# Two pairs of weight sums formed one run earlier, and an empty step ahead of a batch's scores

## The chip, the cores and the metric

The kernel runs on one core of one Trainium2 chip. The metric is the time of one execution on the device in microseconds (us), lower is better. Times of a kernel are the median of several runs; traces come from one profiled execution.

## The reference

Eight batches with 8 heads, 576 tokens and a head dimension of 64. Keys and values are averaged over groups of 8 tokens, the attention is formed over the 72 averages, and its result (4608 tokens by 512) goes through a feed-forward layer 512 -> 2048 -> 512 with a leaky ReLU of slope 0.01. All in float32.

```python
k_p = k.reshape(B, H, Sp, pool, D).mean(axis=3)
v_p = v.reshape(B, H, Sp, pool, D).mean(axis=3)
scores = scale * np.matmul(q, k_p.transpose(0, 1, 3, 2))
scores = scores - np.max(scores, axis=-1, keepdims=True)
attn = np.exp(scores)
attn = attn / (np.sum(attn, axis=-1, keepdims=True) + 1e-09)
attn_out = np.matmul(attn, v_p)
...
h = x @ w_in
g = np.maximum(0.01 * h, h)
return (g @ w_out).astype(np.float32)
```

## The kernel before, in words

**Work.** The feed-forward layer takes the tokens in nine chunks of 512 (the four tiles of 128 of a chunk). Every factor is split into a high and a low part, so a product takes three matmuls. `m1` (L1131) forms one block of 128 of the 2048 hidden columns for a chunk: 12 matmuls (L1143 to L1145) into a bank `ph` of which there are two in turn, Prelu on ScalarE (L1148), the high part `gh` on ScalarE (L1151), the low part `gl` on VectorE (L1152). `m2` (L1156) adds such a block, two blocks later, to the four accumulators `acc`: 12 matmuls (L1354 to L1356 in `add_up`). Between two `yield`s lie six matmuls; this is a beat.

**Runs.** `runs` lists twelve stretches: run 0 is chunk 0 with hidden blocks 0 to 7, runs 1 and 2 chunk 1 with blocks 0 to 7 for half the tiles each, run 3 chunk 1 with blocks 8 to 15, run 4 (`REST`) chunk 0 with blocks 8 to 15, which is the first chunk's second half, and runs 5 to 8 are the third to the sixth chunk whole. The last three chunks are computed by another scheme with seven products in place of eight, which needs sums and differences of quarters of the weights. For each of eight pairs of hidden blocks these sums are formed beforehand and kept in DRAM (`kept`) by `prepare` (L1172).

**prepare.** A pair takes seven steps with nine additions on VectorE (L1183) into a scratch tile `x_tail`, four casts to the high part on ScalarE (`high`, L1186) and four differences for the low part on VectorE (`low`, L1190). The eight parts lie in `places`, which `free` (L1223) gives: upper halves of the columns of the x tiles (`xh`, `xl`) of a chunk that is not filled yet. Behind the seventh step eight transfers of 128 KB (L1217) and, for the first few pairs, one of 256 KB (L1220) write them to `kept` from SP's queue. `PLAN` (L1513) says for each run how many pairs it forms, from which beat and until which.

**Attention beside it.** The attention of the next batches is cut into steps that are issued between the beats: `ku` makes the pooled keys transposed (`kT`, L484 and L489, VectorE), `q` the queries (L565), `s` the scores of half the heads of a tile (`pss`, L600) with the maximum (L608, VectorE) and the exps (L610, ScalarE), `sb` the normalised rows `at` (L640 and L641 on VectorE, L644 and L650 on GpSimd, called POOL in the profile), which SP writes to DRAM (`rows`, L661) and reads back in another layout (`blocks`, L670). `pu` transposes the blocks (`pp`, L681, VectorE) and splits them (`pT_hi` L703 on ScalarE, `pT_lo` L706 and a masked `pT_hi` L710 on VectorE), `au` multiplies by the values (`pa`, L725 to L728) and copies the result to the x tiles (`xh` L744, `xl` L745). A batch's tiles go through `pu` and `au` in pieces. The first twelve steps of batch 2 are put at the end of run 3 (L1499), behind twelve empty steps.

**Outputs.** When a tile of a run has all its blocks, `store` (L1394 and around) copies its accumulator to `o`, one half on ScalarE and one on VectorE, and SP stores it; buffers `o` and `pp` share a pool of five.

**Order.** TensorE's instructions are issued in the order in which the program is written. Up to the last three chunks the order on the other engines and on SP is set by a scheduler, from dependences and estimated times.

Of the kernel before, what the change touches and what calls it, by code (L numbers as in the profile page):

```python
# [10 lines left out]
F32 = mybir.dt.float32  # L11
# [13 lines left out]
def tile_pooled_attention_ffn(  # L25
# [9 lines left out]
    nc = tc.nc  # L35
# [36 lines left out]
    HALF = CH // 2  # L72
# [679 lines left out]
    def x_parts(c):  # L752

        if c not in xs:
            side = c if c < 2 else (c + 1) % 2
            xs[c] = [
                [one.tile([P, CH], F32R, tag=f"x{w}{side}_{kk}", name=f"x{w}{c}_{kk}") for kk in range(NK)]
                for w in "hl"
            ]
        return xs[c]  # L760
# [285 lines left out]
    def line_up_pinned(pieces, ahead, fresh):  # L1046
# [73 lines left out]
    runs = [  # L1120
        (0, range(SPLIT), FULL), (1, range(SPLIT), FULL[:2]), (1, range(SPLIT), FULL[2:]),
        (1, range(SPLIT, NF), FULL), (0, range(SPLIT, NF), FULL),
    ]
    REST = len(runs) - 1
# [45 lines left out]
    kept = dram.tile([len(PAIRS), P, 5, 2, HALF], F32, name="kept")  # L1170

    def prepare(j, places):  # L1172

        f0, f1 = PAIRS[j]
        (a11, a12), (a21, a22) = (
            [[ws[0, f].bitcast(F32)[:, part, half] for part in range(2)]
             for half in (slice(0, HALF), slice(HALF, DM))] for f in (f0, f1)
        )
        u, w = (x_tail[:, 2 * i : 2 * i + 2, :].rearrange("p k x -> p (k x)") for i in range(2))
        ADD, SUB = ALU.add, ALU.subtract  # L1180

        def do(out, a, b, op):
            nc.vector.tensor_tensor(out, a, b, op=op)  # L1183

        def high(i, of):
            nc.scalar.copy(places[i][0], of)  # L1186

        def low(i, of):
            h, l = places[i]
            nc.vector.tensor_tensor(l, of, h.bitcast(F32), op=SUB)  # L1190

        do(u, a21[0], a21[1], ADD)
        do(w, u, a22[0], ADD)
        yield
        do(w, w, a22[1], ADD)
        high(1, w)
        do(u, a11[0], u, SUB)
        yield
        do(u, u, a11[1], ADD)
        high(0, u)  # L1200
        low(1, w)
        yield
        do(w, w, a11[0], SUB)
        low(0, u)
        yield
        do(w, w, a11[1], SUB)
        high(2, w)
        do(u, a12[0], w, SUB)
        yield
        do(u, u, a12[1], ADD)  # L1210
        high(3, u)
        low(2, w)
        yield
        low(3, u)
        for i, parts_of in enumerate(places):
            for k, part in enumerate(parts_of):
                nc.sync.dma_start(kept[j, :, i, k, :], part.bitcast(F32))  # L1217
        if j < OPEN:
            with tc.issue_after(sent[-1].ins):
                nc.sync.dma_start(kept[j, :, 4], ws[0, f1].bitcast(F32)[:, :, HALF:])  # L1220
        yield

    def free(n, i):  # L1223

        if n < REST + FAST - 2:
            return [(h[:, HALF:], l[:, HALF:]) for h, l in zip(*x_parts(runs[n][0] + 1))]
        side, part = (runs[n][0] + 2) % 2, "hl"[i % 2]
        x = [one.tile([P, CH], F32R, tag=f"x{part}{side}_{kk}", name=f"place{i}_{kk}") for kk in range(NK)]
        return [(y[:, :HALF], y[:, HALF:]) for y in x]
# [251 lines left out]
    for n, pieces in enumerate(beside):  # L1481
        us = [att[b][u] for b, u in line_up([x for x in pieces if x[0] < VIA])]
        us += [
            att[x[0]][x[1]] if x else lambda: None
            for x in line_of(n, [x for x in pieces if x[0] >= VIA])
        ]
        if n == 0:

            cut = us.index(att[1]["au01"]) + 1
            us, rest = us[:cut], us[cut:]  # L1490

            us.remove(att[1]["sa20"])
            us.insert(us.index(att[1]["au00"]) + 1, att[1]["sa20"])
            us = [att[0][u] for u in TAIL_STEPS.split()] + us
        elif n == 1:
            us = rest
        if n == REST:

            units[-1] = [lambda: None] * AHEAD + us[:AHEAD]  # L1499
            us = us[AHEAD:]  # L1500
        units.append(us)
# [8 lines left out]
    for b, n in loads_at.items():  # L1510
        early[max(n, REST) - 1].append(b)

    PLAN = {REST + 1: (2, 10, 36), REST + 2: (3, 3, 34), REST + 3: (1, 3, 20), REST + 4: (2, 3, 34)}  # L1513
    STEPS_OF = 7
    left = list(range(len(PAIRS)))

    def sums_in(n):
        for i in range(PLAN[n][0]):
            yield from prepare(left.pop(0), free(n, i))

    at = 0
    for n, (c, fs, ts) in enumerate(runs[: REST + FAST - 1]):
        us = list(units[n])
# [12 lines left out]
        beats, done, beat = (2 + len(ts) // 2) * len(fs), 0, 0  # L1536
        forming, formed = (sums_in(n), 0) if n in PLAN else (None, 0)
        many, begin, until = PLAN.get(n, (0, 0, 1))
        behind = 10 if final else 4
# [43 lines left out]
    for part in (at - 2, at - 1):  # L1583
        n, c, f = parts[part]
# [12 lines left out]
    for n in range(REST + FAST - 1, len(runs)):  # L1597
        c = runs[n][0]
        us = list(units[n])
# [61 lines left out]
```

## Time and profile before

| | |
|---|---|
| median of 3 runs | 916.63 us (916.19 to 918.4) |
| the profiled execution | 919.39 us |
| its span in the trace | 917.6 us |
| mean granted TensorE clock | 0.991 |
| TensorE busy | 886.1 us, 97% |
| VectorE / ScalarE / GpSimd busy | 56% / 49% / 24% |

The profile is one execution; its span runs from the first to the last instruction, and the execution's time is 1.8 us longer. In rows of instructions the first two numbers are the start from the span's start and the duration, `<-` stands between what is written and what is read, and in brackets stand the idle time before and what ended it. Matmuls overlap, so that one shows 0.39 us though the next starts 0.23 us after it. The clock is given as a share of 2.4 GHz.

### The profile page before, as it was taken

How to read it: one execution, taken by the hardware profiler on the slowest of the kernel's cores; microseconds unless marked ns; L12 is line 12 of the kernel's file. 1: busy time of each engine (PE TensorE's matmuls, PEld its weight loads, DVE VectorE, ACT ScalarE, POOL GpSimd, SP SyncE). 2: the span in 40 equal slices, each digit the busy share in tenths (PEclk: the TensorE clock that was granted, in tenths of full speed). 3: DMA queues.
4: the chain of work that ended last, by engine and by line, in shares of the span. 5: the costliest groups of instructions: out<-in, count | busy, mean ns of one | idle time of the engine just before them, and what ended most of it. 6: DMA issues, size and time to landing. Idle time of an engine off the chain costs nothing.

```text
span 917.6 us, 14146 instructions
## 1 busy us (share of the span) xinstructions
PE 886.1 (97%) x4731; PEld 764.1 (83%) x4731; DVE 515.8 (56%) x1229; ACT 447.4 (49%) x1397; POOL 223.6 (24%) x394
## 2 busy tenths in 40 slices
PE   5599999999999999999999999999999999999998
PEld 4478888788887888888888888888999999999997
DVE  6999569546276654774465537655665653342222
ACT  5788559345344534443454336354654553453322
POOL 4511110352534231412133132514320230010000
PEclk9889999999999999999999999999999999999999
DMA  9965231327357342834245317630785255425332
GB/s 266 313 203 171 64 76 47 88 61 197 102 163 169 109 96 53 230 93 109 53 141 118 97 36 195 162 102 3 198 212 148 67 148 144 122 78 161 104 113 72
DMA packets 157464, 116.53 MB, mean 127 GB/s; under 512 B 100688, under 2 KB 136016, under 8 KB 157392
## 3 DMA queue, kind: packets, MB, share of 16 engines
q1 hardware_dynamic: 145488, 90.86, 36.7%
q10 hardware_dynamic: 11904, 24.78, 9.4%
q8 instruction: 37, 0.61, 0.3%
q14 instruction: 35, 0.29, 0.1%
HBM read 85.07 MB, written 30.54 MB: 126 GB/s over the span
## 4 chain that ended last, share of the span: by engine, by line
PE 84%; DVE 7%; ACT 3%; DMA 2%; POOL 1%; issue 1%; SPq 1%; POOLq 0%; DVEq 0%; ACTq 0%
PE acc L1354 13%; PE acc L1355 13%; PE acc L1356 13%; PE ph L1143 8%; PE ph L1144 8%; PE ph L1145 8%; PE ends_y L1261 7%; PE ends_x L1261 6%; PE pss L600 3%; DMA kremraw<-in_k_dram 1%; PE pa L726 1%; DMA blocks<-rows 1%; PE pa L728 1%; PE pa L727 1%; PE pa L725 1%
## 5 line engine op out<-in xcount | busy, mean ns | idle before, releaser
L1354 PE MATMUL acc<-w,gh 128*128 128x512 f32 x576 | 228.2, 396 | 0.7 <-DVE o L1394 0.7
L1355 PE MATMUL acc<-w,gh 128*128 128x512 f32 x576 | 225.9, 392 | 0.0
L1356 PE MATMUL acc<-w,gl 128*128 128x512 f32 x576 | 225.0, 391 | 0.0
L1143 PE MATMUL ph<-xh,w 128*128 128x512 f32 (+1 forms) x416 | 159.5, 384 | 0.6 <-DVE gl L1152 0.6
L1144 PE MATMUL ph<-xl,w 128*128 128x512 f32 (+1 forms) x416 | 156.5, 376 | 0.0
L1145 PE MATMUL ph<-xh,w 128*128 128x512 f32 (+1 forms) x416 | 156.3, 376 | 0.0
L1356 PEld LDWEIGHTS acc<-w,gl 128*128 128x128 f32 x576 | 108.4, 188 | 23.5
L1354 PEld LDWEIGHTS acc<-w,gh 128*128 128x128 f32 x576 | 108.7, 189 | 20.1 <-issue 1.1
L1355 PEld LDWEIGHTS acc<-w,gh 128*128 128x128 f32 x576 | 108.7, 189 | 18.1
L610 ACT ACTIVATE e<-pss,red 128x72 f32<-128x72 f32 (+1 forms) x320 | 97.8, 329 | 44.6 <-DVE red L608 44.5
L1148 ACT ACTIVATE ph<-ph 128x512 f32<-128x512 f32 (+1 forms) x104 | 57.7, 555 | 94.8 <-PE ph L1145 94.3
L1152 DVE TENSOR_TENSOR gl<-ph,gh 128x512 fp32r<-128x512 f32 (+1 forms) x104 | 66.8, 642 | 61.3 <-ACT gh L1151 60.8
L644 POOL TENSOR_TENSOR at<-e,red 128x128 f32<-128x128 f32 (+1 forms) x120 | 50.1, 438 | 173.9 <-DVE red L641 90.9
L1143 PEld LDWEIGHTS ph<-xh,w 128*128 128x128 f32 x416 | 79.2, 190 | 14.6 <-DVE gl L1152 1.2
L1145 PEld LDWEIGHTS ph<-xh,w 128*128 128x128 f32 x416 | 79.0, 190 | 14.3
L1144 PEld LDWEIGHTS ph<-xl,w 128*128 128x128 f32 x416 | 79.1, 190 | 13.1
L610 ACT ACTIVATION_READ_ACCUMULATOR e<-pss,red 128x1 f32 (+1 forms) x320 | 68.6, 214 | 0.0
L681 DVE STREAM_TRANSPOSE pp<-blocks 128x384 f32<-128x384 f32 (+1 forms) x60 | 44.2, 758 | 41.2 <-DMA blocks<-rows 41.2
L608 DVE TENSOR_REDUCE red<-pss 128x4 f32<-128x288 f32 (+1 forms) x80 | 35.8, 453 | 52.9 <-PE pss L600 51.5
L703 ACT CAST pT_hi<-pp 128x384 fp32r<-128x384 f32 (+1 forms) x80 | 36.8, 479 | 52.5 <-DVE pp L681 48.7
L1151 ACT CAST gh<-ph 128x512 fp32r<-128x512 f32 (+1 forms) x104 | 57.8, 556 | 2.6
L600 PEld LDWEIGHTS pss<-kT,qT 128*128 128x128 f32 x320 | 45.8, 195 | 8.4 <-ACT qT L577 2.2
(290 smaller groups left out, 1486.2 us busy)
## 6 DMA issues: line engine op xcount, KB each, us to landing
seat<-kept ACTq DMA_DIRECT2D x31, 512.0 KB
rows<-at SPq DMA_DIRECT2D x48, 192.0 KB
blocks<-rows SPq DMA_DIRECT2D x48, 192.0 KB
out_dram<-o SPq DMA_DIRECT2D x34, 256.0 KB
w_bits<-in_moe_w_in_dram SPq DMA_DIRECT2D x16, 512.0 KB
w_bits<-in_moe_w_out_dram SPq DMA_DIRECT2D x16, 512.0 KB
q<-in_q_dram SPq DMA_DIRECT2D x96, 64.0 KB
w<-kept ACTq DMA_DIRECT2D x21, 256.0 KB
```

Of the source, the lines that this page charges most:

```text
L600: nc.tensor.matmul(sc[:, 2 * SP * i : 2 * SP * (i + 1)], qT[:, p, :], kT[:, p, :, :].rearrange("d i s -> d (i s)"), start=True, stop=True,)
L610: ins = nc.scalar.activation(e[:n, h, :], scv[:n, h, :], AF.Exp, bias=mx[:n, h : h + 1], accum_out=sm[:n, h : h + 1],)
L1143: nc.tensor.matmul(ph, w[:, 0, ks], xh[kk][:, r], start=kk == 0, stop=False)
L1144: nc.tensor.matmul(ph, w[:, 0, ks], xl[kk][:, r], start=False, stop=False)
L1145: nc.tensor.matmul(ph, w[:, 1, ks], xh[kk][:, r], start=False, stop=kk == NK - 1)
L1148: nc.scalar.activation(ph, ph, AF.Prelu, alpha=0.01)
L1151: casts.append(nc.scalar.copy(gh, ph))
L1152: lows.append(nc.vector.tensor_tensor(gl, ph, gh.bitcast(F32), op=ALU.subtract))
L1261: nc.tensor.matmul(out, w[:, stay, ks], move, start=start and i + n == 0, stop=i + n == 3, skip_group_check=True,)
L1354: nc.tensor.matmul(a, gh[:, r], hi, start=first, stop=False)
L1355: nc.tensor.matmul(a, gh[:, r], lo, start=False, stop=False)
L1356: nc.tensor.matmul(a, gl[:, r], hi, start=False, stop=last)
```

## The change

Three edits. `low` issues the two transfers of a part right behind its difference, and the eight transfers at the end of `prepare` go; `free` is written so that run 4 too finds the tiles of the next chunk. In run 4's list of attention steps an empty step is inserted at index 2, behind twelve empty ones, so that it lies ahead of the first scores of batch 2. And `PLAN` gives two pairs to run 4 (beats 1 to 14), one instead of two to run 5 (beats 3 to 17 instead of 10 to 36), two instead of three to run 6 (from beat 7 instead of 3); runs 7 and 8 stay.

```diff
@@ prepare
         def low(i, of):
             h, l = places[i]
             nc.vector.tensor_tensor(l, of, h.bitcast(F32), op=SUB)
+            for k, part in enumerate(places[i]):
+                nc.sync.dma_start(kept[j, :, i, k, :], part.bitcast(F32))
...
         low(3, u)
-        for i, parts_of in enumerate(places):
-            for k, part in enumerate(parts_of):
-                nc.sync.dma_start(kept[j, :, i, k, :], part.bitcast(F32))
@@ free
-            return [(h[:, HALF:], l[:, HALF:]) for h, l in zip(*x_parts(runs[n][0] + 1))]
+            return [(h[:, HALF:], l[:, HALF:]) for h, l in zip(*x_parts(n - REST + 2))]
@@ the steps of run 4
         if n == REST:
 
+            us.insert(2, lambda: None)
             units[-1] = [lambda: None] * AHEAD + us[:AHEAD]
             us = us[AHEAD:]
...
-    PLAN = {REST + 1: (2, 10, 36), REST + 2: (3, 3, 34), REST + 3: (1, 3, 20), REST + 4: (2, 3, 34)}
+    PLAN = {REST: (2, 1, 14), REST + 1: (1, 3, 17), REST + 2: (2, 7, 34), REST + 3: (1, 3, 20), REST + 4: (2, 3, 34)}
```

What it does to the order stands below at three places. A row names line, operation, what is written and what is read; the last number of a name is a tile's own and differs between the two kernels.

TensorE, in run 3, where the first scores of batch 2 (`pss_0_0`, `pss_0_1`) stand; before:

```order
L1356 MATMUL acc_3_1694<-w_10_1698,gl_10_1977 128x512
L600 MATMUL pss_0_0_2135<-kT,qT_0_2122 128x144 x2
L600 MATMUL pss_0_1_2145<-kT,qT_0_2122 128x144 x2
L1143 MATMUL ph_13_2155<-xh_0_1073,w_13_1847 128x512
L1144 MATMUL ph_13_2155<-xl_0_1077,w_13_1847 128x512
```

And with the change:

```order
L1355 MATMUL acc_3_1694<-w_10_1698,gl_10_1977 128x512
L1143 MATMUL ph_13_2135<-xh_0_1073,w_13_1847 128x512
L1144 MATMUL ph_13_2135<-xl_0_1077,w_13_1847 128x512
L1145 MATMUL ph_13_2135<-xh_0_1073,w_13_1847 128x512
L1143 MATMUL ph_13_2135<-xh_1_1074,w_13_1847 128x512
L1144 MATMUL ph_13_2135<-xl_1_1078,w_13_1847 128x512
L1145 MATMUL ph_13_2135<-xh_1_1074,w_13_1847 128x512
L600 MATMUL pss_0_0_2142<-kT,qT_0_2122 128x144 x2
L600 MATMUL pss_0_1_2152<-kT,qT_0_2122 128x144 x2
L1143 MATMUL ph_13_2135<-xh_2_1075,w_13_1847 128x512
```

The scores stand six matmuls later, in the middle of `ph_13`. The second tile's move in the same way.

TensorE, at the start of run 4, where the third tile's scores stand; before:

```order
L1145 MATMUL ph_8_2340<-xh_3_394,w_8_1108 128x512
L600 MATMUL pss_2_0_2366<-kT,qT_2_2267 128x144 x2
L600 MATMUL pss_2_1_2376<-kT,qT_2_2267 128x144 x2
L1143 MATMUL ph_9_2386<-xh_0_391,w_9_1193 128x512
L1144 MATMUL ph_9_2386<-xl_0_395,w_9_1193 128x512
```

With the change:

```order
L1145 MATMUL ph_8_2345<-xh_3_394,w_8_1108 128x512
L1143 MATMUL ph_9_2380<-xh_0_391,w_9_1193 128x512
L1144 MATMUL ph_9_2380<-xl_0_395,w_9_1193 128x512
L1145 MATMUL ph_9_2380<-xh_0_391,w_9_1193 128x512
L1143 MATMUL ph_9_2380<-xh_1_392,w_9_1193 128x512
L1144 MATMUL ph_9_2380<-xl_1_396,w_9_1193 128x512
L1145 MATMUL ph_9_2380<-xh_1_392,w_9_1193 128x512
L600 MATMUL pss_2_0_2387<-kT,qT_2_2274 128x144 x2
L600 MATMUL pss_2_1_2397<-kT,qT_2_2274 128x144 x2
L1143 MATMUL ph_9_2380<-xh_2_393,w_9_1193 128x512
```

`ph_9`, which takes the bank that `ph_15` had, now follows `ph_8` directly; the scores come six matmuls later.

VectorE, in run 4, from the low part of the last block of run 3 (`gl_15`) on; `x_tail` is the scratch tile of the sums, `w_0` and `w_4` are weights, `red` the maxima and sums of the softmax. Before:

```order
L1152 TENSOR_TENSOR gl_15_2297<-ph_15_2274,gh_15_2296 128x512
L608 TENSOR_REDUCE red_2_0_2370<-pss_2_0_2366 128x4
L608 TENSOR_REDUCE red_2_1_2380<-pss_2_1_2376 128x4
L565 STREAM_TRANSPOSE qT_4_2838<-q_4_2269 128x2x4x32
L1152 TENSOR_TENSOR gl_8_2363<-ph_8_2340,gh_8_2362 128x512
L640 TENSOR_TENSOR red_2_0_2370<-red_2_0_2370,tiny 128x4
L641 RECIPROCAL red_2_0_2370<-red_2_0_2370 128x4
L640 TENSOR_TENSOR red_2_1_2380<-red_2_1_2380,tiny 128x4
L641 RECIPROCAL red_2_1_2380<-red_2_1_2380 128x4
L1152 TENSOR_TENSOR gl_9_2401<-ph_9_2386,gh_9_2400 128x512
L681 STREAM_TRANSPOSE pp_0_0_2428<-blocks_0_0_2426 128x4x96
L1394 COPY o_0_2415<-acc_0_1381 128x256
```

With the change:

```order
L1152 TENSOR_TENSOR gl_15_2289<-ph_15_2267,gh_15_2288 128x512
L1183 TENSOR_TENSOR x_tail<-w_0_336 128x256
L1183 TENSOR_TENSOR x_tail<-x_tail,w_0_336 128x256 x2
L1183 TENSOR_TENSOR x_tail<-w_4_657,x_tail 128x256
L1183 TENSOR_TENSOR x_tail<-x_tail,w_4_657 128x256
L1190 TENSOR_TENSOR xl_1_2329<-x_tail,xh_1_2325 128x256
L1152 TENSOR_TENSOR gl_8_2365<-ph_8_2345,gh_8_2364 128x512
L1183 TENSOR_TENSOR x_tail<-x_tail,w_4_657 128x256
L1190 TENSOR_TENSOR xl_0_2328<-x_tail,xh_0_2324 128x256
L608 TENSOR_REDUCE red_2_0_2391<-pss_2_0_2387 128x4
L608 TENSOR_REDUCE red_2_1_2401<-pss_2_1_2397 128x4
L565 STREAM_TRANSPOSE qT_4_2890<-q_4_2276 128x2x4x32
```

Between `gl_15` and `gl_8` stand five sums and a difference of the first pair, behind it more; up to the last `pT_hi` of the first piece (`pp_1_0`) it is ten sums and four differences, and `gl_10` has come ahead of that too.

ScalarE at the same place, before:

```order
L1151 CAST gh_15_2296<-ph_15_2274 128x512
L1148 ACTIVATE ph_8_2340<-ph_8_2340 128x512
L1151 CAST gh_8_2362<-ph_8_2340 128x512
L610 ACTIVATE e_2_0_2369,red_2_0_2370<-pss_2_0_2366,red_2_0_2370 128x72 x4
L610 ACTIVATE e_2_1_2379,red_2_1_2380<-pss_2_1_2376,red_2_1_2380 128x72 x4
L1148 ACTIVATE ph_9_2386<-ph_9_2386 128x512
```

With the change:

```order
L1151 CAST gh_15_2288<-ph_15_2267 128x512
L1186 CAST xh_1_2325<-x_tail 128x256
L1186 CAST xh_0_2324<-x_tail 128x256
L1148 ACTIVATE ph_8_2345<-ph_8_2345 128x512
L1151 CAST gh_8_2364<-ph_8_2345 128x512
L610 ACTIVATE e_2_0_2390,red_2_0_2391<-pss_2_0_2387,red_2_0_2391 128x72 x4
L610 ACTIVATE e_2_1_2400,red_2_1_2401<-pss_2_1_2397,red_2_1_2401 128x72 x4
L1148 ACTIVATE ph_9_2380<-ph_9_2380 128x512
L1186 CAST xh_2_2326<-x_tail 128x256
L1392 COPY o_0_2429<-acc_0_1381 128x256
```

Two casts of the first pair (L1186) stand ahead of `ph_8`'s Prelu, a third ahead of the first output copy.

## Rows read from the trace of the kernel before

**Rows 1.** The page: the span, and each engine's busy time in us.

```profile
span 917.6 us, 14146 instructions
...
PE 886.1 (97%) x4731; PEld 764.1 (83%) x4731; DVE 515.8 (56%) x1229; ACT 447.4 (49%) x1397; POOL 223.6 (24%) x394
```

**Rows 2.** TensorE's waits, 160 to 640 us: us in total, times, longest.

```profile
PE pa L726 <- DVE pT_lo L706: 2.1, 1, 2.1
PE pss L600 <- DVE kT L489: 1.1, 1, 1.1
PE acc L1354 <- DVE o L1394: 0.7, 1, 0.7
```

**Rows 3.** Windows: us, busy PE, PEld, DVE, ACT, POOL; clock, DMA share, GB/s.

```profile
182.00:184.00 2.00, 0.89 (x7) 0.74 (x7) 1.88 (x7) 0.00 (x0) 0.60 (x1) 1.00 1.00 227
207.04:218.11 11.07, 11.07 (x54) 9.31 (x53) 8.23 (x20) 7.69 (x28) 2.85 (x8) 1.00 0.79 213
290.00:292.00 2.00, 0.15 (x2) 0.00 (x0) 2.00 (x5) 0.46 (x2) 2.00 (x5) 1.00 0.49 155
292.00:294.00 2.00, 1.71 (x10) 1.51 (x11) 2.00 (x5) 0.43 (x1) 0.99 (x3) 0.84 0.73 209
294.00:296.00 2.00, 2.00 (x6) 1.63 (x5) 1.84 (x6) 0.39 (x2) 0.00 (x0) 0.50 0.68 138
296.00:298.00 2.00, 2.00 (x8) 1.60 (x8) 0.85 (x2) 1.97 (x7) 0.00 (x0) 0.81 0.75 207
```

**Rows 4.** The chain of waits into two stalls: start, us on the chain, what.

```profile
283.20 4.47 DMA blocks<-rows
...
364.68 3.33 DMA out_dram<-o
...
369.76 0.23 PE acc L1356
```

**Rows 5.** Timeline of TensorE: start, us, instruction, idle before and its releaser.

```profile
183.29 1.22 PE L600 MATMUL pss<-kT,qT 128*128 128x144 f32 x8 [1.11 <-DVE kT L489]
...
207.15 1.14 PE L600 MATMUL pss<-kT,qT 128*128 128x144 f32 x8
208.03 0.49 PE L1143 MATMUL ph<-xh,w 128*128 128x512 f32 x1
...
219.03 0.28 PE L725 MATMUL pa<-pT_hi,v_hi 128*128 128x256 f32 x1
```

**Rows 6.** Timeline of VectorE.

```profile
185.90 1.24 DVE L640 TENSOR_TENSOR red<-red,tiny 128x4 f32<-128x4 f32 x1
...
207.04 0.69 DVE L1152 TENSOR_TENSOR gl<-ph,gh 128x512 fp32r<-128x512 f32 x1 [0.16 <-ACT gh L1151]
...
289.05 1.38 DVE L1190 TENSOR_TENSOR xl<-x_tail,xh 128x256 fp32r<-128x256 f32 x1
...
294.69 0.89 DVE L1183 TENSOR_TENSOR x_tail<-x_tail,w 128x256 f32<-128x256 f32 x2
295.49 0.42 DVE L1183 TENSOR_TENSOR x_tail<-w,x_tail 128x256 f32<-128x256 f32 x1
...
297.76 0.42 DVE L1183 TENSOR_TENSOR x_tail<-x_tail,w 128x256 f32<-128x256 f32 x1
298.09 0.42 DVE L1190 TENSOR_TENSOR xl<-x_tail,xh 128x256 fp32r<-128x256 f32 x1
```

**Rows 7.** Timeline of ScalarE.

```profile
206.38 0.63 ACT L1151 CAST gh<-ph 128x512 fp32r<-128x512 f32 x1
207.35 0.58 ACT L1148 ACTIVATE ph<-ph 128x512 f32<-128x512 f32 x1 [0.34 <-PE ph L1145]
207.96 0.59 ACT L1151 CAST gh<-ph 128x512 fp32r<-128x512 f32 x1
...
295.61 0.41 ACT L1186 CAST xh<-x_tail 128x256 fp32r<-128x256 f32 x1 [3.18 <-DVE x_tail L1183]
```

**Rows 8.** Timeline of GpSimd.

```profile
185.83 1.29 POOL L265 TENSOR_TENSOR v1raw<-v1raw 128x512 f32<-128x512 f32 x1 [0.34 <-DMA v1raw<-in_v_dram]
```

## The prediction, made before the changed kernel had run

> **What bounds the kernel now.** I read the page first: TensorE is busy 886.1 of 917.6 us, 97% [rows 1]. So the time is TensorE's own work, which the change does not touch (the same 4227 rows in its stream), plus the moments at which it stands. Second, the waits of TensorE from 160 us to 640 us, where the change does its work: three that matter [rows 2], 2.1 us at `pa` for `pT_lo` (near 290 us, in the third chunk), 1.1 us at the scores for `kT` (at 183.29 us, end of run 3) and 0.7 us at `acc` for an output copy (near 368 us). Third, the windows around the longest of them: from 290 to 292 us TensorE is busy 0.15 us while VectorE is busy 2.00 of 2.00, and afterwards the granted clock is 0.84, 0.50 and 0.81 in three windows of 2 us [rows 3]. 0.50 is the lower of its two levels, 1.2 of 2.4 GHz; what it did before the fall was to stand for 2.1 us. In the window that holds the 1.11 us gap, 182 to 184 us, it stays at 1.00. Fourth, the chain into two of the stalls: a 4.47 us transfer of `blocks` that starts at 283.20, behind it sums and differences of a pair on VectorE, and a 3.33 us store of an output tile whose buffer the copy at 368 us had to wait for [rows 4].
>
> The sum is made against the profiled execution, 919.39 us; the median of the three runs is 916.63, lower by 2.76. So I work out a difference and put it on the median. About 0.3% (2.75 us) is what a measurement of this kernel can tell from no change.
>
> **Part 1, the empty step.** It puts the first three tiles' scores of batch 2 one beat (six matmuls) later. At the first, `kT` comes 1.11 us too late now [rows 5]; six matmuls of 0.23 us [rows 4] lie in front then, 1.36 us with their fractions,, so that gap of **1.1** goes. But the third tile's scores also leave their place between `ph_8` and `ph_9`. `ph_9` writes the bank that `ph_15` had, so it needs `gl_15`, which starts at 207.04 and takes 0.69 [rows 6]: 207.73. Now `ph_8` ends at 207.15, the scores fill 0.88 us, and `ph_9` starts at 208.03 [rows 5] with nothing to wait for. `gl_15` itself comes no earlier, as ScalarE reaches its cast (206.38, [rows 7]) only behind the exps of the second tile, whose scores move a beat later (1.36) and 1.1 earlier: 0.25, which I leave out. `ph_8` then ends at 207.15 - 1.11 = 206.04 and TensorE waits 1.7 us. Part 1 by itself: -1.1 + 1.7 = **+0.6**, bounds -1.1 (if `gl_15` moves along) and +0.6.
>
> **Part 2, two pairs in run 4.** In VectorE's new order ten sums (L1183) and four differences (L1190) stand between `gl_15` and the last `pT_hi` of the first piece. In the window from `gl_15`'s start to the end of that `pT_hi`, 207.04 to 218.11, VectorE worked 8.23 of 11.07 us [rows 3]; with 0.3 us between instructions I call it 8.5. A sum that needs the one before costs 0.40 (two in 0.80, from 294.69 to 295.49), another sum or a difference 0.33 to 0.34 (297.76 to 298.09) [rows 6]: 7 x 0.40 + 7 x 0.33 = 5.1 us. `gl_10` too now stands ahead of the last pair of `pT`, 0.6. Waits come on top. ScalarE does the casts of the first two sums ahead of `ph_8`'s Prelu. The second of them needs the fifth sum, five sums after 207.73, so 209.5; its cast takes 0.41 (at 295.61), Prelu and cast of `ph_8` 0.6 each (207.35, 207.96) [rows 7]: `gh_8` is there at 211.1, while VectorE is through with all ahead of it at 209.8: it waits 1.25. The first output copy stands behind `ph_9`'s Prelu and a third cast on ScalarE and so holds VectorE's half back by some 0.85 us; the exps I count as covered by two sums and `qT`. So the last `pT_hi` ends at 207.0 + 8.5 + 5.1 + 0.6 + 2.1 = **223.3**, instead of 218.1. TensorE reached `pa` at 219.03 [rows 5]; one beat later and 0.5 late from part 1 it is there at 220.9. It waits 2.4, in one piece or before it at the output copies. Bounds of this term: 0 (if the backlog fits) and 4.8 (with two blocked instructions at 1.2 us). Parts 1 and 2: **+3.0**.
>
> What hides the rest: the second pair's 10 sums left stand beside `m1` and `m2` with no one waiting; if `gl` fell behind them, `m2` would stand. The new transfers go out earlier, 8 of 128 KB a pair from SP's queue, and blocks and rows of batch 2 stand behind some of them. ScalarE's copies of `pa` (L744) write columns in which the second pair's results lie until its transfers have read them. No row of before shows such a wait; bounds 0 and the 4.47 us of a transfer [rows 4], and I take 0, since what those copies write is first read a chunk later.
>
> **Part 3, one pair fewer in run 5, and early.** The run now forms one pair between beats 3 and 17 instead of two between 10 and 36. Run 5 begins near 254 us (`ph_8` starts 2.7 us before 207.15; eight parts of 24 matmuls of 0.23 us follow, and some 5 us of scores and `pa`), and a beat is 1.36 us, so the sums are past by some 278 us and none stands between the arrival of `blocks` and the `pT`. VectorE then has no 1.38 us difference at 289.05 [rows 6] in the way, and `blocks` stand behind fewer transfers. The 2.1 us stall goes, and with it what the clock costs afterwards: 2 x (0.16 + 0.50 + 0.19) = 1.7. **-3.8**, bounds -3.8 and 0.
>
> **Part 4, two pairs in run 6, from beat 7 on and not 3.** The output copies of run 5 fall on beats before the sums, so the store that held the buffer for 3.33 us starts some 2 us sooner [rows 4]: **-0.7**, bounds -0.7 and 0. Runs 7 and 8 keep one and two pairs; all eight are made by the same point.
>
> Sum: +3.0 - 3.8 - 0.7 = **-1.5** for the profiled run (917.9), and on the median 916.63 - 1.5 = **915.1**. That is inside what can be told apart from no change.
>
> One row speaks against the change: beside POOL at 185.83 (1.29 us) a VectorE operation of 128x4, with little to do, took 1.24, and both ended near 187.1 [rows 6, 8]. I count no such case in run 4.
>
> The Trainium skill, "SBUF — State Buffer", section "SBUF: two separate sides", says that VectorE and GpSimd hold a shared pair of ports in turn: a VectorE instruction with two inputs in SBUF against a GpSimd instruction that reads SBUF, and whichever began first keeps the pair to its end. The sums have two such inputs, and the 185.90 row agrees with it. By that rule the moved sums would stretch wherever GpSimd forms `at`, which is the third rival.
>
> **The rivals.**
> *Absorbed.* Run 4 costs only part 1's 0.6: ScalarE and VectorE have waits enough. For it: 2.84 of 11.07 us without work [rows 3]. Against: 5.1 added. 0.6 - 3.8 - 0.7 = -3.9, so 912.7. Decides: whether the last `pT_hi` comes before 221.
> *The clock falls in run 4.* The stalls of 1.7 and 2.4 us follow each other by 12 us; after 2.1 us at 290 it went to 0.50, after 1.1 us at 183 it stayed at 1.00 [rows 3]. Decides: which of the two a stall of 2.4 us is like. The fall costs 1.7: +0.2, so 916.8.
> The Trainium skill, "TensorE: Matmul & The Clock Gate", section "A second HAM failure mode: psum-queue depth-cycling", tells of short idles between groups of matmuls that make the clock swing; by it the two stalls here would make this rival the likely one; the windows at 290 us fit it, that at 183 us does not.
> *Ports* (ends slower). In run 4, between `gl_15` and the last `pT`, GpSimd works 2.85 us [rows 3] on the third tile's `at`. If three sums or differences stand behind it for 1.0 us each (1.38 less 0.42 at 289.05 against 298.09, [rows 6]), the wait at `pa` is 5.4 and the clock falls: 3.0 + 3.1 + 1.7 - 4.5 = +3.3, so 919.9. Decides: whether that wait passes some 2 us more than I have.
> *The third chunk's stall stays.* SP's queue is taken in order, and a kept transfer waiting for its difference stands in front of `blocks_3_0`: only -0.7 is saved: +3.0 - 0.7 = +2.3, so 918.9. For it: four transfers of the pair are issued near. Against: they wait only for sums of beat 17 at the latest. Decides: whether `blocks_3_0` still arrives after 287.
>
> **The numbers.** Forecast 0.40, absorbed 0.25, clock 0.15, ports 0.12, stall stays 0.08. Most of absorbed (0.23) and a third of the forecast (0.14), whose bounds reach below 913.9, are faster by over 0.3%: 0.37. Over 919.4 lie 0.08 of ports, 0.04 of the stall that stays, 0.06 of clock and forecast together with a blocked instruction: 0.18. Between: 0.45. The range is 911.0 (absorbed, with part 1 at its lower bound: 912.7 - 1.7) to 919.9 (ports).
>
> **What would show it.** Right: no gap at the first scores; `ph_9` waiting about 1.7 us for `gl_15`; the last `pT` of the first piece near 223 and a wait of 2 us at its `pa`; no stall at 290 us, clock 1.00 there; none at 368. Wrong: a wait for `pT` in run 4 under 0.5 us or over 4, a clock under 0.9 anywhere in run 4, a `blocks` wait in the third chunk, or a wait on `gl` in run 5 or 6.

## The result: slower, 924.48 us against 917.54

Six runs of each kernel on the same chips: the changed kernel has a median of 924.48 us (921.79 to 925.55), the kernel before 917.54 (916.19 to 920.16). The ratio is 1.0065, with a 95% interval of 1.005 to 1.0081. So the change made the kernel some 0.65% slower. The forecast was 915.1, and its range ended at 919.9 with the rival *Ports*, whose mechanism is not what happened. The profiled execution of the changed kernel took 924.99 us.

The page of the changed kernel, the span and the engines' busy time, to set beside [rows 1]. Its line numbers are one lower from the transfers of `prepare` on, so that L1353 is L1354 of before:

```profile
span 923.1 us, 14143 instructions
...
PE 888.1 (96%) x4731; PEld 763.6 (83%) x4731; DVE 517.9 (56%) x1229; ACT 447.6 (48%) x1397; POOL 221.4 (24%) x394
```

TensorE does the same 4731 matmuls. Its waits from 160 to 640 us, which answer to [rows 2]:

```profile
PE ph L1143 <- DVE gl L1152: 6.1, 5, 2.7
PE acc L1353 <- DVE o L1393: 1.1, 2, 0.7
PE pa L726 <- DVE pT_lo L706: 0.2, 1, 0.2
```

The waits at the scores and at the third chunk's `pa` are gone; the 0.2 us at `pa` lie elsewhere, in run 4. In their place stand five waits of `ph` for `gl`, 6.1 us in all, where the kernel before had one of 0.2, at 590.80 us. The timeline of TensorE (start, us, instruction, idle before and its releaser) shows where all of them lie:

```profile
207.47 0.50 PE L1143 MATMUL ph<-xh,w 128*128 128x512 f32 x1 [1.13 <-DVE gl L1152]
...
218.68 0.50 PE L1353 MATMUL acc<-w,gh 128*128 128x512 f32 x1 [0.73 <-DVE o L1393]
220.71 0.49 PE L1353 MATMUL acc<-w,gh 128*128 128x512 f32 x1 [0.37 <-DVE o L1393]
223.59 0.38 PE L726 MATMUL pa<-pT_lo,v_hi 128*128 128x256 f32 x1 [0.24 <-DVE pT_lo L706]
...
266.14 0.50 PE L1143 MATMUL ph<-xh,w 128*128 128x512 f32 x1 [0.74 <-DVE gl L1152]
...
292.87 0.50 PE L1143 MATMUL ph<-xh,w 128*128 128x512 f32 x1 [2.69 <-DVE gl L1152]
...
402.83 0.50 PE L1143 MATMUL ph<-xh,w 128*128 128x512 f32 x1 [0.73 <-DVE gl L1152]
...
596.33 0.50 PE L1143 MATMUL ph<-xh,w 128*128 128x512 f32 x1 [0.81 <-DVE gl L1152]
```

The idle time in brackets is less than what a wait costs, since a matmul shows 0.39 us where the next starts 0.23 us after it, and since the clock may fall. To price each place I set the start of the n-th matmul of one trace against the n-th of the other (the same number in both) and read how the difference changes:

| stretch of the kernel before, us | changed kernel less before, us | what lies there |
|---|---|---|
| 174 to 188 | -1.36 | the gap at the first scores is gone |
| 201 to 214 | +1.75 | `ph_9` waits for `gl_15` |
| 214 to 227 | +2.74 | output copies and `pa` of run 4's first piece |
| 251 to 264 | +1.04 | `ph` waits for `gl`, start of run 5 |
| 276 to 306 | +0.60 | third chunk: the old stall gone, a new one in its place |
| 357 to 370 | -0.92 | the wait for an output copy is gone |
| 397 to 409 | +1.03 | `ph` waits for `gl`, fourth chunk |
| 586 to 600 | +0.60 | `ph` waits for `gl`, sixth chunk: 0.81 us idle, 0.21 before |

With +0.05 from the beginning they add up to 5.5, the difference of the spans.

The third chunk is where the forecast had its gain. The chain of waits of the changed kernel there (start, us on the chain, what; `SPq` is SP issuing a transfer):

```profile
287.05 0.66 SPq L288
...
287.80 3.62 DMA blocks<-rows
...
291.44 0.04 DVE pp L681
...
292.14 0.68 DVE gl L1152
...
292.87 0.50 PE ph L1143
```

In the kernel before [rows 4] `blocks` had also come late, at 287.67, and then sums stood ahead of the `pT` that `pa` needed. But `gl_4` had run ahead of the wait for them, on VectorE:

```profile
283.06 0.69 DVE L1152 TENSOR_TENSOR gl<-ph,gh 128x512 fp32r<-128x512 f32 x1 [0.73 <-ACT gh L1151]
...
287.76 1.07 DVE L681 STREAM_TRANSPOSE pp<-blocks 128x384 f32<-128x384 f32 x2 [3.68 <-DMA blocks<-rows]
```

Now no sum stands there, and TensorE does not get as far as `pa`: `ph_6` needs the bank of `gl_4`, and `gl_4` stands on VectorE behind a transpose `pp` that waits for these same `blocks`. VectorE's rows in the changed kernel say it directly; `gl_4` sits out the idle time of 4.56 us ahead of `pp` as well:

```profile
291.44 0.86 DVE L681 STREAM_TRANSPOSE pp<-blocks 128x384 f32<-128x384 f32 x1 [4.56 <-DMA blocks<-rows]
292.14 0.67 DVE L1152 TENSOR_TENSOR gl<-ph,gh 128x512 fp32r<-128x512 f32 x1
```

And the clock fell again behind the wait, as in [rows 3] (windows: length, busy PE, PEld, DVE, ACT, POOL, clock, DMA share, GB/s):

```profile
290.00:292.00 2.00, 0.18 (x1) 0.00 (x0) 0.56 (x1) 0.00 (x0) 1.13 (x3) 1.00 1.04 259
292.00:294.00 2.00, 1.13 (x4) 0.94 (x5) 2.00 (x6) 1.36 (x4) 1.57 (x4) 0.87 1.07 192
294.00:296.00 2.00, 2.00 (x7) 1.52 (x6) 2.00 (x3) 0.58 (x1) 1.96 (x3) 0.50 0.62 157
```

The order of VectorE's instructions, before and now (the low parts `gl` and the transposes `pp` alone, third chunk and fourth chunk):

```
third chunk,  before:  gl_3 gl_4 pp_3_0 pp_4_0 pp_3_1 gl_5 pp_4_1 gl_6
third chunk,  changed: gl_3 pp_3_0 gl_4 pp_4_0 gl_5 pp_3_1 pp_4_1 gl_6
fourth chunk, before:  gl_4 pp_3_0 gl_5 pp_4_0 gl_6 pp_3_1 pp_4_1 gl_7
fourth chunk, changed: gl_4 gl_5 pp_3_0 pp_4_0 pp_3_1 pp_4_1 gl_6 gl_7
```

In both chunks the change has let the scheduler put a `pp` ahead of a `gl` that it used to follow. Such an order can be read before a kernel runs, as those of runs 3 and 4 were; the prediction had not looked at these two chunks.

### The profile page after: what moved, and what is told of

It is laid out like the page before. It is cut to its first block, busy times and chain, and to the rows that moved or that the text cites. A ratio compares the mean times of both kernels' runs of the same rounds, so it can differ in the third digit from the quotient of the medians.

```text
span 923.1 us, 14143 instructions
## 1 busy us (share of the span) xinstructions
PE 888.1 (96%) x4731; PEld 763.6 (83%) x4731; DVE 517.9 (56%) x1229; ACT 447.6 (48%) x1397; POOL 221.4 (24%) x394
## 4 chain that ended last, share of the span: by engine, by line
PE 74%; DVE 8%; DMA 6%; ACT 4%; POOL 3%; SPq 2%; issue 2%; POOLq 0%; DVEq 0%; ACTq 0%
PE acc L1353 11%; PE acc L1354 11%; PE acc L1355 11%; PE ends_y L1260 7%; PE ph L1143 7%; PE ph L1145 7%; PE ph L1144 7%; PE ends_x L1260 6%; PE pss L600 3%; ACT e L610 2%; DMA blocks<-rows 2%; DMA kremraw<-in_k_dram 1%; DVE x_tail L1183 1%; SPq L318 1%; PE pa L726 1%
## 5 line engine op out<-in xcount | busy, mean ns | idle before, releaser
L1353 PE MATMUL acc<-w,gh 128*128 128x512 f32 x576 | 228.0, 396 | 1.2 <-DVE o L1393 1.1
L1354 PE MATMUL acc<-w,gh 128*128 128x512 f32 x576 | 225.4, 391 | 0.0
L1353 PEld LDWEIGHTS acc<-w,gh 128*128 128x128 f32 x576 | 108.6, 188 | 21.6 <-DVE o L1393 2.5
L1354 PEld LDWEIGHTS acc<-w,gh 128*128 128x128 f32 x576 | 108.5, 188 | 18.0
```

The lines of the kernel that those rows point to most:

```text
L1353: nc.tensor.matmul(a, gh[:, r], hi, start=first, stop=False)
L1354: nc.tensor.matmul(a, gh[:, r], lo, start=False, stop=False)
```

## The experiments

Theories at the start: A, that run 4's transfers stand in SP's queue ahead of the third attention batch's loads and make all later steps late; B, that VectorE's additional work in run 4 does it; C, that the empty step unsettles the order. Behind the first four runs came G, that the order of `gl` and `pp` does it, against L, that the blocks are late whatever the order. "Of before" means runs of the kernel before on the same chip. In the experiments with a rule the line numbers are one higher from the edit on.

**1. The empty step alone.**

```diff
 (kernel before)
+            us.insert(2, lambda: None)
```

> The kernel before with the empty step alone. Theory A (SP's queue: the transfers of the two pairs of run 4 stand ahead of the third attention batch's loads) and theory B (VectorE's additional work in run 4) both expect nothing of note: the 1.1 us gap at 183 us goes, a wait for gl of 1.1 to 1.7 us comes at 207, in all within 1 us of before. Theory C (the step itself unsettles the scheduler's order) expects waits for gl after 260 us, 2 us or more slower.

Measured: ratio to before 0.9999 (0.9989 to 1.001). Its trace has no gap at the first scores, the wait of `ph_9` that the first step of the prediction had named, and a smaller stall in the third chunk:

```profile
208.53 0.50 PE L1143 MATMUL ph<-xh,w 128*128 128x512 f32 x1 [1.13 <-DVE gl L1152]
293.41 0.39 PE L726 MATMUL pa<-pT_lo,v_hi 128*128 128x256 f32 x1 [1.71 <-DVE pT_lo L706]
```

By the matmuls' starts the gap at 183 us gives 1.39 us back and `ph_9` costs 1.98. C falls: no wait for `gl` near 266 or 402. The third chunk is 2.04 us cheaper than in the trace of before, with the same order there; experiment 9 comes back to that.

**2. The change without the empty step.**

```diff
 (changed kernel)
-            us.insert(2, lambda: None)
```

> The changed kernel without the empty step. Theories A and B: the waits for gl at 266, 292, 402 and 596 us stay, 4 to 7 us slower than before. Theory C: they go, within 1 us of before plus run 4's own waits (3 us).

Measured: 1.0086 (1.0071 to 1.0102), no better than the change. Run 4 costs 7.7 us here in place of 4.5 (201 to 239 us), most of it at `pa`; the waits near 292, 402 and 596 us are there (1.51, 0.37 and 0.57 us), against C, and that near 266 is not. So by the traces the empty step is a help to run 4 with sums in it, which the prediction had not seen, as it judged the step by itself.

**3. Run 4's transfers from another queue.**

```diff
 (changed kernel)
-                nc.sync.dma_start(kept[j, :, i, k, :], part.bitcast(F32))
+                (nc.scalar if j < 2 else nc.sync).dma_start(kept[j, :, i, k, :], part.bitcast(F32))
```

> The changed kernel, with the 16 transfers of run 4's two pairs issued from ScalarE's queue in place of SP's; the order of the computing instructions stays. Theory A: the loads of k for batch 3 start near 219 instead of 224 us, the loads of the remainder of v near 240 instead of 247, the waits at 266 and 292 shrink to under 0.5 and 1 us, 3 to 5 us faster than the changed kernel. Theory B: nothing changes (VectorE does the same work), within 1 us of the changed kernel. Rival D (the DMA engines are full from 216 to 234 us, whichever queue asks): the loads start earlier but land no earlier, gain under 1 us.

Measured: 1.01 (1.0074 to 1.0127), no faster than the change. The load of k for batch 3 in SP's queue, first of the changed kernel, then here:

```profile
223.99 1.31 SPq L288 DMA_DIRECT2D k0raw<-in_k_dram  x2
```

```profile
223.50 2.03 SPq L288 DMA_DIRECT2D k0raw<-in_k_dram  x2
```

With the eight of the transfers that stood ahead of it gone it starts 0.5 us sooner, not 5: it also stands behind the output stores and the rows of scores, and these wait for VectorE and ScalarE. The wait in the third chunk stays, 1.92 us at 297.60. So A falls for these two. It does not fall for the load of v's remainder, which starts at 244.08 and not 247.50 us, nor for the wait near 266, which is not there in this run. The trace cannot tell more than this, as ScalarE itself is now held by the transfers (3.4 us ahead of one `gh`).

**4. The third step alone.** One pair in run 5 from beat 3 to 17, the other goes to run 7; nothing in run 4.

```diff
 (kernel before)
-    PLAN = {REST + 1: (2, 10, 36), REST + 2: (3, 3, 34), REST + 3: (1, 3, 20), REST + 4: (2, 3, 34)}
+    PLAN = {REST + 1: (1, 3, 17), REST + 2: (3, 3, 34), REST + 3: (2, 3, 34), REST + 4: (2, 3, 34)}
```

> The kernel before with one pair fewer in run 5 (one from beat 3 to 17), which goes to run 7, and nothing in run 4: the third step of the prediction by itself. If that step was right and only run 4's transfers spoiled it (theory A): no stall of over 0.5 us near 290 us, 2 to 4 us faster than before. If the third chunk's stall has another cause (what SP has ahead of the blocks of the fourth tile: loads that wait for GpSimd): a stall of 1.5 us or more near 290 stays, within 1.5 us of before.

Measured: 0.9994 (0.9985 to 1.0004): no gain. This is the run that turned the study. With run 4 untouched the third chunk has the stall of the changed kernel, a wait for `gl` behind a `pp`; VectorE, then TensorE:

```profile
286.27 0.85 DVE L681 STREAM_TRANSPOSE pp<-blocks 128x384 f32<-128x384 f32 x1 [5.55 <-DMA blocks<-rows]
286.98 0.67 DVE L1152 TENSOR_TENSOR gl<-ph,gh 128x512 fp32r<-128x512 f32 x1
```

```profile
287.70 0.50 PE L1143 MATMUL ph<-xh,w 128*128 128x512 f32 x1 [1.96 <-DVE gl L1152]
```

Run 4 (A and B) is not needed for it. From here on G and L.

**5. The fourth step alone.** Run 6 with two pairs from beat 7.

```diff
 (kernel before)
-    PLAN = {REST + 1: (2, 10, 36), REST + 2: (3, 3, 34), REST + 3: (1, 3, 20), REST + 4: (2, 3, 34)}
+    PLAN = {REST + 1: (2, 10, 36), REST + 2: (2, 7, 34), REST + 3: (2, 3, 34), REST + 4: (2, 3, 34)}
```

> The kernel before with run 6 forming two pairs from beat 7 (one pair goes to run 7): the fourth step by itself. Theory G (VectorE's new order puts gl_6 of the fourth chunk behind four pp that wait for blocks): no stall at 369 us (0.7 to 0.9 us less) but a wait for gl of 0.5 to 1 us near 400 us; within 1 us of before. Rival R (that wait comes from the lateness that run 4 brings): no wait near 400, 0.7 to 1 us faster.

Measured: 1.001 (0.9996 to 1.0024). The stall at 369 us is gone, 0.60 us by the matmuls' starts, and a wait for `gl` of 0.30 us at 397.85 costs 0.60: as much is lost as won. The sign is G's, the size smaller than it had said.

**6. Run 4's pairs spread over beats 1 to 30.** In this kernel the second pair's parts are written into columns of the third chunk's x until 254 us, while the attention results come there from 222 us on, so part of that chunk is computed from other numbers. In the changed kernel the parts were done at 229 us, and the results came from 230 on.

```diff
 (changed kernel)
-    PLAN = {REST: (2, 1, 14), ...
+    PLAN = {REST: (2, 1, 30), ...
```

> The changed kernel with run 4's two pairs spread over beats 1 to 30 in place of 1 to 14. If the sums that VectorE has ahead of the first piece's pT make run 4's cost (4.5 us from 201 to 227 us): half of them are gone from there, the output copies and pa wait under 1 us together in place of 1.5, run 4's cost falls to 2 to 3 us, 1.5 to 2.5 us faster than the changed kernel. If the waits come from the new places of ScalarE's casts and of the scores: no change.

Measured: 1.0108 (1.0087 to 1.013). Seven sums and two differences stand ahead of the first piece's last `pT_hi` here, not ten and four; it ends at 222.38 us, not at 223.79, and the stretch from 214 to 227 us costs 1.0 us in place of 2.7. So the sums do price that stretch. The total says nothing of it, since `pa` of the second piece now waits 4.29 us until columns of x are free.

**7. One pair in run 4.**

```diff
 (changed kernel)
-    PLAN = {REST: (2, 1, 14), REST + 1: (1, 3, 17), REST + 2: (2, 7, 34), ...
+    PLAN = {REST: (1, 1, 14), REST + 1: (1, 3, 17), REST + 2: (3, 3, 34), ...
```

> The changed kernel with one pair in run 4 (beats 1 to 14) and three from beat 3 in run 6. If run 4's cost comes from the number of sums ahead of the first piece's pT: about half of the 4.5 us, 2 to 2.5 us faster there than the changed kernel; the wait near 402 us goes, as run 6 is as before, and the one at 369 us comes back; near 292 us all stays. In all 2 to 3.5 us faster than the changed kernel. If the cost comes from the places of the scores and casts: run 4 unchanged.

Measured: 1.0034 (1.0019 to 1.005), 3 us faster than the change, but not for the reason given. From 214 to 227 us it costs 2.77, as the change did (2.74), and from 201 to 214 us 1.07 in place of 1.75. Eight sums and three differences stand ahead of the last `pT_hi`, but also a `pp` of 0.83 us that used to follow, and it ends at 223.65. The miss has the same root as the main one: with another plan the order is another. What it gains besides lies in the third chunk (a wait of 1.86, not 2.69) and in no wait near 266 and 402.

**8. Every `pp` behind the `gl` issued before it**, in the changed kernel and, in a second run, in the kernel of experiment 4.

```diff
 def turn_via
-        pin(nc.vector.transpose(...))
+        with nullcontext() if pinned else tc.issue_after(lows[-1].ins):
+            pin(nc.vector.transpose(...))
```

> The changed kernel, with every pp (the transpose of blocks) kept behind the gl that was issued before it in the program, as it was in the kernel before near 290 us. Theory G (a pp that waits for late blocks stands ahead of a gl on VectorE, and ph waits for that gl): the waits for gl at 292, 402 and 596 us go, the slow clock behind the first with it, pa near 293 waits 0.5 us at most: 4 to 5.5 us faster than the changed kernel. Rival L (the blocks are late whatever the order): a wait for pT of 1.5 us or more takes the place of the one at 292, less than 2 us faster.

> The kernel before with one pair in run 5 from beat 3 to 17 (the other goes to run 7), and every pp behind the gl issued before it. Theory G: the third step was right but for the order: no stall near 290 us, clock 1.00 there, 3 to 4 us faster than before. Rival L: a stall of 1.5 us or more at pa near 290 us, within 1.5 us of before.

Measured: 1.0196 (1.0165 to 1.0228) and 1.0254 (1.0236 to 1.0272), both far slower, 11.0 and 23.5 us by the medians than the same kernels without the rule, against both theories' numbers. The rule was too wide: everywhere else a `pp` that used to slip in early is held, and `pa` waits for it (the first of the two, TensorE's waits):

```profile
PE pa L726 <- ACT pT_hi L704: 9.9, 7, 3.1
PE pa L727 <- DVE pT_lo L707: 3.1, 4, 1.2
PE ph L1144 <- DVE gl L1153: 1.1, 1, 1.1
```

But the waits for `gl` at 266, 292, 402 and 596 us are gone, and from 276 to 306 us the two kernels are 3.0 and 3.2 us cheaper than before. G had the place right, so the rule was cut down to it.

**9. The rule for one `pp` alone** (the first half of the heads of batch 2's fourth tile, which falls in the third chunk), in the kernel of experiment 4, then in the changed kernel, then in that with a second `pp` of the fourth chunk held behind `gl_6`.

```diff
 def turn_via
-        pin(nc.vector.transpose(...))
+        with tc.issue_after(lows[-1].ins) if (b, t, g) in ((2, 3, 0),) else nullcontext():
+            pin(nc.vector.transpose(...))
 (third kernel: in ((2, 3, 0), (3, 4, 0)))
```

> The kernel before with one pair in run 5 from beat 3 to 17 (the other in run 7), and one rule: in the third chunk the first pp behind gl_4, as it was in the kernel before; no other pp is held. Theory G: the third step of the prediction comes out: no stall over 0.7 us near 290 us, no slow clock, 3 to 4 us faster than before. Rival L (late blocks whatever the order): a wait for pT of 1.5 us or more near 290, within 1.5 us of before.

> The changed kernel with the same one rule in the third chunk. Theory G: the 2.7 us wait for gl near 292 us and the slow clock behind it go, at most 1 us of waiting for pT comes in their place: 3 to 4.5 us faster than the changed kernel, so 920 to 921.5; the waits near 266, 402 and 596 us stay. Rival L: 1.5 us or more at pa, less than 2 us faster.

> As the one before, and in the fourth chunk pp of the last tile behind gl_6. Theory G: the wait for gl near 402 us goes too, another 0.7 to 1 us. Rival R (the sums and the late blocks keep VectorE busy there in any order): a wait of the same size at pa behind it.

Measured: the first 0.9973 (0.9962 to 0.9983), faster than both kernels, 916.63 us where runs of before on that chip had 918.4 (the 916.63 of before's first three runs is the same number by chance). That is 2.5 us, less than the 3 to 4 that G had said. The second 920.49 us, 1.0027 (1.0014 to 1.0039), 4.0 us faster than the changed kernel by the medians and 3.5 by the ratios, as G had said. The third 920.47 us, 1.0016 (1.0003 to 1.0028), within the noise of the second.

The second of them is the plain test, since SP's queue stands as in the changed kernel and the blocks come at the same time. VectorE and TensorE there:

```profile
287.25 0.69 DVE L1153 TENSOR_TENSOR gl<-ph,gh 128x512 fp32r<-128x512 f32 x1 [0.28 <-ACT gh L1152]
291.46 1.32 DVE L682 STREAM_TRANSPOSE pp<-blocks 128x384 f32<-128x384 f32 x2 [3.52 <-DMA blocks<-rows]
```

```profile
294.94 0.39 PE L727 MATMUL pa<-pT_lo,v_hi 128*128 128x256 f32 x1 [0.57 <-DVE pT_lo L707]
```

`pp` starts at 291.46 us, as in the changed kernel (291.44). `gl_4` starts at 287.25 and not 292.14. TensorE works through and waits 0.57 us at `pa`, where the changed kernel waited 2.69, and its clock stays:

```profile
290.00:292.00 2.00, 2.00 (x10) 1.69 (x9) 0.54 (x1) 0.00 (x0) 1.74 (x5) 1.00 0.99 255
292.00:294.00 2.00, 2.00 (x10) 1.65 (x10) 1.80 (x5) 1.61 (x4) 0.96 (x2) 1.00 1.06 200
```

L falls: the blocks are as late, and the stall is gone. In the first kernel of the three TensorE has no wait there at all; these are all its waits from 160 to 660 us:

```profile
PE pss L600 <- DVE kT L489: 0.8, 1, 0.8
PE ph L1144 <- DVE gl L1153: 0.8, 1, 0.8
PE acc L1355 <- DVE o L1395: 0.3, 1, 0.3
```

The third has no wait near 402 us any more, 1.0 us in the trace; its median is the same as the second's, so of that the timing shows nothing. It has the same order as the second up to there and shows no wait near 266 us, the second 0.41, the changed kernel 0.74: that wait comes and goes between executions. So does the one near 596: 0.21 us before, 0.94 in experiment 10, which has the plan of before, and 1.18 in this third kernel.

What the third chunk costs, by the matmuls' starts from 276 to 306 us, against the trace of before:

| order there | kernels | less than before, us |
|---|---|---|
| `gl_4` first, sums between `pp` and `pT` | experiments 1, 5, 10 | 2.0, 0.4, 2.9 |
| `pp` first, no sums | the change, 2, 3, 4, 6, 7 | -0.6, 2.2, 0.2, 0.1, 0.0, 1.9 |
| `gl_4` first, no sums | 8 (two), 9 (three), 11 | 3.0, 3.2, 4.0, 3.1, 3.4, 4.0 |

These are single executions, and the medians move less. From experiment 4 to the first kernel here the rule alone brings 3.9 us in the table and 1.9 by the ratios (0.9994 and 0.9973): the trace of experiment 4 is the slowest of its ten executions, 920.26 us.

**10. The early transfers alone**, the second edit.

```diff
 (kernel before; in low, and no longer at the end of prepare)
+            for k, part in enumerate(places[i]):
+                nc.sync.dma_start(kept[j, :, i, k, :], part.bitcast(F32))
```

> The kernel before with the transfers issued behind each difference alone (plan and steps as before). Theory G (only the order of gl and pp on VectorE matters in the third chunk, and the transfers' place does not): the stall near 290 us stays or shrinks by under 1 us, within 1 us of before. Rival T (the early transfers themselves put blocks later in SP's queue): the stall near 290 grows by 1 us or more, slower by 1 to 3 us.

Measured: 0.9999 (0.9989 to 1.0009). T falls. Its stall in the third chunk is 0.82 us, a larger drop than G had allowed for:

```profile
291.13 0.38 PE L726 MATMUL pa<-pT_lo,v_hi 128*128 128x256 f32 x1 [0.82 <-DVE pT_lo L706]
```

Its trace is 2.9 us cheaper there than the trace of before, but its median is no better. So the trace of before shows an execution in which that stall was dear (2.14 us and the slow clock); experiments 1 and 5, with the same order there, had 1.71 and 1.78.

**11. The third and fourth steps with the two rules**, nothing in run 4, three pairs in run 7.

```diff
 (kernel before, with the rule for (2, 3, 0) and (3, 4, 0))
+    PLAN = {REST + 1: (1, 3, 17), REST + 2: (2, 7, 34), REST + 3: (3, 3, 34), REST + 4: (2, 3, 34)}
```

> The kernel before with run 5's one pair from beat 3 to 17, run 6's two from beat 7, three in run 7, and the two rules (gl_4 ahead of pp in the third chunk, gl_6 ahead of the last tile's pp in the fourth): steps three and four of the prediction without run 4's sums. Theory G: neither stall, near 290 nor near 369 or 402 us: 4.5 us faster than before in the trace (3.8 + 0.7). Rival: three pairs in run 7 bring a wait for gl of 0.5 us or more there, 3.5 us faster or less.

Measured: 1.0002 (0.999 to 1.0014). Both steps show in the trace, 4.0 us from 276 to 306 and 0.9 from 357 to 370. Then run 7 takes 3.7 back in one wait of 1.9 us and the slow clock behind it. Its chain has sums, differences, `pT` and two `pp` ahead of the `gl`:

```profile
494.32 1.03 DVE pp L682 x2
495.35 0.53 DVE gl L1153
...
495.93 0.50 PE ph L1144
```

So the rival came true: three pairs in run 7 bring a wait for `gl` there. The kernel to keep is the first of experiment 9.

## Why the prediction was wrong

The forecast for the profiled execution was -1.5 us, and the spans differ by +5.5. Of these 7.0 us the third chunk has 4.4, the `gl` of the fourth 0.8 net, the waits near 266 and 596 us 1.6 and run 4 0.1. So with part 3 right the sum would still have been some 1 us slower than before, and not faster; the changed kernel with that one order put back is slower too (experiment 9, 1.0027).

**Parts 1 and 2, run 4: right in sum.** Forecast +0.6 for the empty step and +3.0 with the sums; measured 0.6 (1.98 less 1.39, experiment 1) and 3.1 (1.75 and 2.74 less 1.36). The last `pT_hi` of the first piece, forecast to end at 223.3 us, ends at 223.79:

```profile
223.46 0.33 DVE L710 SCALAR_TENSOR_TENSOR pT_hi<-pp,marks,pT_hi 128x128 fp32r<-128x128 f32 x1
```

Of the stretch's wait, the most lay at the output copies (0.73 and 0.37 us) and little at `pa` (0.24), where the prediction had looked for 2 us and had called less than 0.5 a sign of being wrong. Nor does the empty step's price stand by itself: without the step run 4 costs more, not less, once the sums are there (experiment 2). Experiment 7 shows that the count of sums is not a price by itself: three instructions fewer, and another moved in.

**Part 3, the third chunk: the step that failed.** That the 2.1 us stall goes, and with it what the clock costs afterwards, was forecast as -3.8 and measured +0.6: in its place `ph_6` waited 2.69 us for `gl_4`, and the clock fell to 0.50 again. Its reason, that no sum stands between the blocks and `pT`, is true of the changed kernel, and would have been enough had `gl_4` stayed ahead of `pp`: with that one order put back, experiment 9 has 3.1 to 4.0. What the step left out is what would be late next once the stall was gone. That was the blocks themselves, and the first instruction behind them on VectorE was `gl_4`. Nor did the blocks come much sooner. They landed 3.8 us later than before (291.42 against 287.67), with TensorE 4.2 us behind by then, which is a gain of 0.4 against TensorE. From 284.43 to 287.80 us SP issues a store of rows, two transfers of sums and two loads for the next batch ahead of them. The step had counted the transfers of sums and not looked at what else stands there.

The size was off as well. The 3.8 us were the price of one execution; experiments 1, 5 and 10 put the same stall between 1.1 and 3.6 us, and the kernel without it (experiment 9, the first) gained 2.5 us by its ratio (0.9973 of 918.4), where its trace gained 3.9.

**Part 4: right, and paid back.** Forecast -0.7, measured -0.92. But the plan also put all four `pp` ahead of `gl_6` in the fourth chunk, where two had stood, +1.03; experiment 5 shows the same with nothing in run 4. The prediction named a wait on `gl` in run 5 or 6 as what would prove it wrong, and gave it no chance and no price.

**The rest.** The waits near 266 and 596 us (+1.04, +0.60) had no term. That near 266 is ScalarE's exps ahead of a Prelu, behind the late sum of v's remainder; it costs 0 to 1 us between executions of kernels that have the same order up to there (experiment 9). That near 596 varies as much, with the plan of before too; its cause stays open. The wait that the prediction took at nothing, of the copies of `pa` for transfers out of the same columns, did not come in run 4 of the changed kernel; with the pairs spread it did, 4.29 us (experiment 6).

**The rivals.** *Absorbed* is out: the backlog cost what was worked out. *The clock falls in run 4* did not come, though four waits follow each other within 17 us. No single stall of 2.4 us came either, which was this rival's condition. The windows there:

```profile
206.00:208.00 2.00, 0.87 (x4) 0.49 (x3) 1.74 (x5) 0.69 (x2) 0.83 (x3) 1.00 0.80 166
...
218.00:220.00 2.00, 1.32 (x6) 1.05 (x6) 2.00 (x6) 1.00 (x2) 1.12 (x3) 1.00 1.03 328
...
222.00:224.00 2.00, 1.76 (x9) 1.13 (x8) 2.00 (x6) 0.51 (x1) 0.00 (x0) 1.00 0.93 299
```

The Trainium skill, "TensorE: Matmul & The Clock Gate", section "A second HAM failure mode: psum-queue depth-cycling", tells of short idles that recur between groups of matmuls and make the clock swing. Four waits of 0.24 to 1.13 us in a row did not do it in these windows. *Ports*: no sum or difference in run 4 was blocked for a microsecond (its sum takes 3.1 us for three instructions at 1.0, 0.1 too many, which changes nothing). *The stall stays* had the place right, and its sign, blocks after 287 us, came. The mechanism was wrong: it was given 0.08 for SP's queue, and with the blocks as late the order on VectorE alone took the stall away (experiment 9).

## What to carry to other kernels

When a change moves work on one engine under a scheduler, compare the order of all steps that the critical engine waits for, over the whole span that the change touches, and look in particular for an instruction that waits for a transfer and now stands ahead of one that TensorE needs. Removing the work behind a late transfer gains nothing if the transfer's first reader blocks the engine anyway; one ordering rule at that place did, while the same rule everywhere cost 11 and 23 us. And price a stall from several executions: one trace had this one at 4.0 us, others with the same order there at 1.1 to 3.6.

## What was not expected of the hardware

Whether the clock falls behind a stall was not a matter of its length alone. In the third chunk it fell behind 1.78 us in experiment 5 and behind 1.96 in experiment 4, and not behind 1.71 in experiment 1 nor 1.86 in experiment 7. The windows at the end of the stall and behind it, of experiment 5 and of experiment 7:

```profile
292.00:294.00 2.00, 1.75 (x10) 1.61 (x11) 2.00 (x6) 0.38 (x1) 0.94 (x3) 0.88 0.70 204
294.00:296.00 2.00, 2.00 (x6) 1.52 (x6) 1.80 (x6) 0.43 (x2) 0.00 (x0) 0.50 0.68 155
```

```profile
290.00:292.00 2.00, 1.15 (x5) 0.98 (x6) 2.00 (x7) 1.38 (x4) 1.59 (x4) 1.00 0.92 170
292.00:294.00 2.00, 2.00 (x11) 1.65 (x10) 2.00 (x3) 0.66 (x2) 1.94 (x3) 1.00 0.62 164
```

A stall of some 1.8 us there cost 1.9 to 2.2 us without the fall and 3.6 to 3.9 with it, by the matmuls' starts (4.0 less the table's figures). What decides is not shown by the runs.

Beside GpSimd's work a small VectorE step took far longer than elsewhere, in the third chunk of the changed kernel (VectorE, then GpSimd):

```profile
294.00 2.04 DVE L710 SCALAR_TENSOR_TENSOR pT_hi<-pp,marks,pT_hi 128x64 fp32r<-128x64 f32 x1
```

```profile
293.71 1.01 POOL L356 TENSOR_SCALAR k_rem<-kremraw,sides 64x64 f32<-64x64 f32 x2
294.69 2.08 POOL L265 TENSOR_TENSOR v0raw<-v0raw 128x512 f32<-128x512 f32 x2
```

The same step took 2.04 us in experiment 4 too, and 0.28 us in the first kernel of experiment 9. GpSimd worked 1.96 of 2.00 us from 294 to 296 us in the changed kernel (the window shown with the result). The Trainium skill, "SBUF — State Buffer", section "SBUF: two separate sides", has the two engines hold a pair of ports in turn, whichever began first for its whole instruction. The rows agree in that the step began while GpSimd was at work and lasted until 296.04 us, as GpSimd went on. But by the recorded starts the GpSimd instruction of 294.69 us began 0.69 us after the step and still went ahead of it, which is not the order that the section gives. Whether the ports were the cause, no run here tests. It cost TensorE nothing here, as it had work.
